# Loads alternating between the queues of SP and ACT in a decode kernel that streams 346 MB

## The chip, the cores and the metric

The kernel runs on one core of a Trainium2 chip. The core has five engines: TensorE (PE) for matrix products, VectorE (DVE), ScalarE (ACT), GpSimd (POOL) and SyncE (SP), which here only issues transfers. Each engine works through its own list of instructions in order and waits on semaphores for the others. Transfers between the large memory and the on-chip memory are issued by an engine into a queue that belongs to it (SP's is q1 in the profile, ACT's is q10) and are carried out by 16 DMA engines that all queues share. A transfer of 128 rows raises its semaphore by 16 when all its rows have landed.

The metric is the device time of one execution in microseconds (us). Lower is better.

## The reference

One token is decoded. Its vector x (1024 numbers) goes through two branches, and a scalar gate mixes them:

```
g = sigmoid(sum(x * gate_w))
a = attention(x): q = x @ wq; 32 query heads share 4 key/value heads,
                  65536 cached keys and values of 128 numbers each;
                  softmax(q k / sqrt(128)) v, then @ wo
b = x + sigmoid(x @ w_r) * ((silu(x @ w_gate) * (x @ w_up)) @ w_down)
out = g * a + (1 - g) * b
```

Everything is float32. The caches of keys and values are 4 x 65536 x 128 numbers each, 134 MB apiece; the weights are the rest. Each number is used for one token only, so the work per byte is small.

## The kernel before

All large inputs are laid out by the host as one stream of 42 loads, in the order of use. Each of the 4 groups (one key/value head with its 8 query heads) has 9 loads of 8 MB: 128 partitions with one contiguous row of 64 KB each. A load holds two units: `wq` and the key chunk 0, then key chunks 1 to 7, then value chunks 0 to 7, then `wo`, 18 units in 9 loads. Six loads of 128 rows of 56 KB follow for the feed-forward branch (gate, up, down); the last two are cut into eight pieces of falling size (`ENDS`).

Three buffers (`stream`, `BUFS = 3`) take the loads in turn. SP walks the loads in order: load i goes to buffer i % 3 and, from the fourth on, waits until PE is done with the load that was there. PE says so by counting up the semaphore `marked`; `MARK` gives the count of each named point. `LAST` names the point that frees each of a group's nine loads: `s0` (key chunk 0 done) for the first, then `s2`, `s4`, `s6`, `v0` (value chunk 0), `v2`, `v4`, `v6`, `w`.

The order of work in one group, all of it written out by hand:

- PE multiplies x by `wq` (L310, mark `q`), DVE copies the result (L229), PE turns it with a small matrix `half` (L317, mark `qt`), DVE spreads it into `qp` (L233).
- For each key chunk c PE computes scores (L326, mark `s`c), ACT copies them out (L171), DVE takes the maximum (L240).
- Maximum over the group (L332 on PE), ACT computes eight exponentials (L176), DVE transposes them (L255), PE multiplies by the values (L338, marks `v`c).
- PE sums and multiplies by `wo` (L345 to L355, marks `o` and `w`).

Before the first group, ACT issues two small loads: `xk` (L161: x, gate_w and w_r, 128 rows of 96 bytes) and, after POOL has cleared its destination (semaphore `x0`), `x_row` (L163: x once more as two rows of 2 KB). DVE waits for `xk`, prepares `xp` and the dot products (L205 to L208); then, in this order in its list, it computes the gates (L211 to L215), waits for `x_row` (semaphore `x2`), scales it (L217), makes the small selection matrices `sel`, `sel4`, `half`, `halves`, `sel8`, `nsel` (L220 to L226), and only then enters the loop over the groups, which begins with the copy of the queries (L229). The scaled `x_row` itself is used first at the end of the attention (L265).

At the end the gate and up products, their activation (ACT, L179) and the down product follow, and SP stores the output.

Of the kernel before, what the change touches and what calls it, by code (L numbers as in the profile page):

```python
# [10 lines left out]
G = 4  # L11
# [16 lines left out]
PER = UNITS // 2  # L28
BUFS = 3

TAIL = 14336
NTAIL = 3 * KB * F // TAIL

ENDS = {NTAIL - 2: [8 * D, TAIL], NTAIL - 1: [6 * D, 10 * D, 12 * D, 13 * D, 13 * D + 768, TAIL]}

PIECES = [(0, 192), (192, NQ)]

EARLY = 24

# [4 lines left out]
MARK = {m: i + 1 for i, m in enumerate(MARKS)}  # L44

LAST = ["s0", "s2", "s4", "s6", "v0", "v2", "v4", "v6", "w"]
# [5 lines left out]
def gated_mix_kernel(nc, x, vecs, heads, ffn, out):  # L52
# [21 lines left out]
    pe, act, dve, pool, sp = nc.tensor, nc.scalar, nc.vector, nc.gpsimd, nc.sync  # L74

    stream = [nc.alloc_sbuf_tensor(f"st{b}", [P, 2 * CH], F32, align_bytes=256)[:, :] for b in range(BUFS)]
# [24 lines left out]
    gate = sig[:, 0:1]  # L101
# [12 lines left out]
    sems = {n: nc.alloc_semaphore(n) for n in names}  # L114
    nums = sorted(s.num for s in sems.values())
    assert nums == list(range(nums[0], nums[0] + len(nums)))


    ends = []
    for i in range(G * PER + NTAIL):  # L120
        b = i % BUFS
        if i >= BUFS:
            g, l = divmod(i - BUFS, PER)
            sp.wait_ge(sems["marked"], MARK[f"{LAST[l]} {g}" if g < G else ["gate 0", "gate 1", "up 0"][l]])
        if i < G * PER:
            sp.dma_start(stream[b], heads[i]).then_inc(sems[f"ld{b}"], 16)
        elif i - G * PER not in ENDS:
            sp.dma_start(stream[b][:, :TAIL], ffn[i - G * PER]).then_inc(sems[f"ld{b}"], 16)
        else:
            cuts = ENDS[i - G * PER]  # L130
            for c0, c1 in zip([0] + cuts, cuts):
                sp.dma_start(stream[b][:, c0:c1], ffn[i - G * PER, :, c0:c1]).then_inc(sems[f"end{len(ends)}"], 16)  # L132
                ends.append((i, c0, c1))
# [23 lines left out]
    def tell(ins, name):  # L157
        acted.append(name)
        return ins.then_inc(sems["acted"])

    act.dma_start(xk, vecs).then_inc(sems["x1"], 16)  # L161
    act.wait_ge(sems["x0"], 1)
    act.dma_start(  # L163
        x_row[:64:32, :], x.rearrange("(f n) -> f n", f=2)
# [3 lines left out]
    for g in range(G):  # L168
        for c in range(NCH):
            act.wait_ge(sems["marked"], MARK[f"s{c} {g}"])  # L170
            tell(act.activation(scores[:, c, :], ps_s[c % 2], AF.Copy), f"s{c} {g}")  # L171
        act.wait_ge(sems["d2a"], g + 1)
        for c in range(NCH):
            t = scores[:, c, :]
            tell(
                act.activation(t, t, AF.Exp, bias=nb, scale=SCALE, accum_out=sums[:, c : c + 1]), f"e{c} {g}"  # L176
            )
    act.wait_ge(sems["marked"], MARK["gate 1"])
    tell(act.activation(hid.rearrange("p (e n) -> p e n", e=2), ps_f[:, :, :FN], AF.Exp, scale=-1.0), "hid")  # L179
    act.wait_ge(sems["marked"], MARK["first"])  # L180
    c0, c1 = PIECES[0]
    tell(act.activation(fin[:, c0:c1], banks[0][:, : c1 - c0], AF.Copy), "first")
# [11 lines left out]
    def after(mark):  # L194
        dve.wait_ge(sems["marked"], MARK[mark])
# [82 lines left out]
    after("last")  # L278
    c0, c1 = PIECES[1]
    dve.tensor_copy(fin[:, c0:c1], banks[1][:, : c1 - c0]).then_inc(sems["d2s"])  # L280
# [8 lines left out]
    def take(name, n=1):  # L289
        pe.wait_ge(sems[name], n).then_inc(sems[name], -n)  # L290
# [106 lines left out]
    for b in range(EARLY, FB):  # L397
        if b == EARLY + 2:
            take("d2p")
        for bank, (c0, c1) in zip(banks, PIECES):  # L400
            n = c1 - c0
# [45 lines left out]
```

## Time and profile before

| | |
|---|---|
| runs of the kernel | 805.68, 805.76, 806.18 us; median 805.76 |
| the profiled execution | 805.78 us, of which the span of the profile is 804.5 us |
| read from the large memory | 346.05 MB, 430 GB/s over the span |
| busy PE, DVE, ACT, POOL | 407.5, 72.3, 44.8, 2.5 us |

Times in the profile are microseconds from the start of the span. "SPq" and "ACTq" are the issues of transfers by these engines; their time is that of the issue alone, not of the transfer. In an instruction's row, the bracket at the end gives the idle time of its engine before it and what ended it. A row that stands for several instructions has their count (x32). The granted clock is the share of its full speed that TensorE was given.

### The profile page before, as it was taken

The numbers are of one execution on the slowest core, as the hardware profiler recorded it, in microseconds if no ns is written. First come the engines' busy times: TensorE is split into PE (matmuls) and PEld (weight loads), VectorE is DVE, ScalarE is ACT, GpSimd is POOL, SyncE is SP. The second block draws the span as 40 slices with busy tenths as digits, with TensorE's granted clock in tenths as the row PEclk, the third lists the DMA queues.
The fourth block names the chain that finished last, engine by engine and source line by source line (L and its number), as shares of the span: only waits on it lengthen the run. The fifth ranks groups of instructions, "written<-read, shape, count | busy, mean of one in ns | idle before, by whom it ended". The sixth has DMA issues, their size and how long they took to land. (4 is left out here: it accounts for less than half of the span.)

```text
span 804.5 us, 6124 instructions
## 1 busy us (share of the span) xinstructions
PE 407.5 (51%) x2826; PEld 122.0 (15%) x2826; DVE 72.3 (9%) x135; ACT 44.8 (6%) x100; POOL 2.5 (0%) x13
## 2 busy tenths in 40 slices
PE   0544464455654564545544454456444545464466
PEld 0211111111111121111111111112111111121122
DVE  0200010000000020000100110000000100000310
ACT  0000030000000030000000110000000300000000
POOL 1000000000000000000000000000000000000000
PEclk9977767768767677677877586777776866787778
DMA  9999999999999999999999999999999999999998
GB/s 418 417 418 466 415 424 460 417 428 453 420 430 450 424 431 446 427 430 446 427 430 443 430 430 443 430 431 430 440 433 427 443 430 430 429 448 426 439 413 342
DMA packets 7078, 346.20 MB, mean 430 GB/s; under 512 B 918, under 2 KB 1050, under 8 KB 1308
## 3 DMA queue, kind: packets, MB, share of 16 engines
q1 hardware_dynamic: 6920, 346.04, 99.4%
q8 instruction: 8, 0.13, 0.1%
q10 hardware_dynamic: 148, 0.02, 0.0%
q14 instruction: 2, 0.02, 0.0%
HBM read 346.05 MB, written 0.00 MB: 430 GB/s over the span
## 5 line engine op out<-in xcount | busy, mean ns | idle before, releaser
L326 PE MATMUL ps_u<-st,qp 128*32 128x512 f32 x1024 | 152.5, 759 | 149.1 <-PEq L290 149.1
L338 PE MATMUL acc<-st,pt 128*32 128x512 f32 x1024 | 152.3, 757 | 144.1 <-PEq L290 144.1
L338 PEld LDWEIGHTS acc<-st,pt 128*32 128x32 f32 x1024 | 43.5, 135 | 250.0 <-issue 250.0
L326 PEld LDWEIGHTS ps_u<-st,qp 128*32 128x32 f32 x1024 | 41.4, 135 | 256.3 <-issue 256.3
L171 ACT ACTIVATE s<-ps_u 128x512 f32<-128x512 f32 x32 | 19.1, 597 | 560.4 <-PE ps_u L326 560.4
L240 DVE TENSOR_REDUCE mx<-s 128x1 f32<-128x512 f32 x32 | 22.0, 686 | 284.2 <-ACT s L171 284.2
L255 DVE STREAM_TRANSPOSE pt<-s 128x512 f32<-128x512 f32 x32 | 22.7, 711 | 198.0 <-PE acc L338 194.4
L310 PE MATMUL ps_u<-st,xp 128*32 128x512 f32 x128 | 23.3, 893 | 22.1 <-PEq L290 22.1
L382 PE MATMUL ps_u<-st,xp 128*32 128x448 f32 x128 | 17.1, 703 | 16.9 <-PEq L290 16.9
L382 PE MATMUL ps_f<-st,xp 128*32 128x448 f32 x128 | 16.8, 691 | 13.3 <-PEq L290 13.3
L176 ACT ACTIVATE s<-s,nb 128x512 f32<-128x512 f32 x32 | 22.6, 708 | 10.4 <-DVE nb L250 10.4
L392 PE MATMUL att<-st,s 128*32 128x512 f32 x96 | 14.9, 776 | 7.5 <-DMA st<-in_ffn 4.9
L355 PE MATMUL att<-st,op 128*32 128x512 f32 x128 | 14.6, 594 | 2.4 <-PEq L290 2.4
L301 PE MATMUL ps_m<-dsum,ones 128*128 128x2 f32 x2 | 0.6, 350 | 23.5 <-PEq L290 23.5
L310 PEld LDWEIGHTS ps_u<-st,xp 128*32 128x32 f32 x128 | 5.9, 158 | 40.1 <-issue 40.1
L382 PEld LDWEIGHTS ps_u<-st,xp 128*32 128x32 f32 x128 | 5.3, 139 | 28.6 <-issue 28.6
L259 DVE COPY s<-acc 128x512 f32<-128x512 f32 x4 | 2.8, 692 | 71.6 <-PE acc L338 71.6
L382 PEld LDWEIGHTS ps_f<-st,xp 128*32 128x32 f32 x128 | 5.2, 135 | 25.1 <-issue 25.1
L229 DVE COPY s<-ps_u 128x512 f32<-128x512 f32 x4 | 2.8, 692 | 53.5 <-PE ps_u L310 53.5
L179 ACT ACTIVATE s<-ps_f 128x896 f32<-128x896 f32 x1 | 0.9, 917 | 105.4 <-PE ps_f L382 105.4
L392 PEld LDWEIGHTS att<-st,s 128*32 128x32 f32 x96 | 3.7, 134 | 18.6 <-issue 10.7
L332 PE MATMUL ps_m<-md,ones 128*128 128x128 f32 x8 | 1.8, 311 | 8.2 <-PEq L290 8.2
(69 smaller groups left out, 68.9 us busy)
## 6 DMA issues: line engine op xcount, KB each, us to landing
st<-in_ffn SPq DMA_DIRECT2D x4, 7168.0 KB, 43.3
st<-in_ffn SPq DMA_DIRECT2D x2, 3072.0 KB, 37.1
st<-in_ffn SPq DMA_DIRECT2D x1, 4096.0 KB, 34.9
st<-in_ffn SPq DMA_DIRECT2D x1, 2048.0 KB, 36.9
st<-in_ffn SPq DMA_DIRECT2D x1, 1024.0 KB, 38.9
st<-in_heads SPq DMA_DIRECT2D x36, 48.1
st<-in_ffn SPq DMA_DIRECT2D x1, 512.0 KB, 39.7
st<-in_ffn SPq DMA_DIRECT2D x1, 384.0 KB, 40.2
```

The source lines that it names most:

```text
L171: tell(act.activation(scores[:, c, :], ps_s[c % 2], AF.Copy), f"s{c} {g}")
L176: act.activation(t, t, AF.Exp, bias=nb, scale=SCALE, accum_out=sums[:, c : c + 1]), f"e{c} {g}"
L229: to_pe(dve.tensor_copy(q_sb, ps_s[0]))
L240: ins = dve.tensor_reduce(mx[:, c : c + 1], scores[:, c, :], AX.X, ALU.max)
L255: to_pe(dve.transpose(pts[:, c % 2, :], scores[:, c, :]))
L259: to_pe(dve.tensor_copy(o_sb, acc.rearrange("p (s d) -> p s d", s=4)))
L310: ins = pe.matmul(ps_s[0][32 * j : 32 * j + 32, :], xp[:, k, :], unit(0)[:, k * D + f * 512 : k * D + (f + 1) * 512], start=(k < 2), stop= ...
L326: ins = pe.matmul(ps_s[c % 2][32 * j : 32 * j + 32, :], qp[:, 32 * s : 32 * s + 32], unit(1 + c)[:, (4 * s + j) * 512 : (4 * s + j + 1) * ...
L338: ins = pe.matmul(acc[32 * j : 32 * j + 32, :], pts[:, c % 2, 32 * m : 32 * m + 32], unit(1 + NCH + c)[:, m * 512 : (m + 1) * 512], start= ...
L355: ins = pe.matmul(att[32 * j : 32 * j + 32, :], op[:, h, :], unit(UNITS - 1)[:, h * D + f * 512 : h * D + (f + 1) * 512], start=False, sto ...
L382: ins = pe.matmul(ps[32 * j : 32 * j + 32, e, :FN], xp[:, k, :], tail((i * KB + k) * F + (2 * j + e) * FN, FN), start=(k == 0), stop=(k == ...
L392: ins = pe.matmul(att[32 * j : 32 * j + 32, :], hp[:, 32 * b : 32 * b + 32], tail(2 * KB * F + b * D + f * 512, 512), start=(b < 2), stop= ...
```

## The change

The loads are dealt out to two queues. Of the first 39 loads (`ONE = 39`) the even ones stay with SP and the odd ones, 1, 3, ..., 37, are issued by ACT. Loads 39 to 41, with all pieces of the end, stay with SP. Buffers, order of use, semaphores and points of release are the same; both queues wait for the same marks as before, load by load.

In ACT's list an odd load's issue stands at these places: load 1 between the issues of `xk` and `x_row`, without a wait; a load that is released by a mark `s`c directly after ACT's copy of that chunk, whose wait for the mark serves both; a load released by `v`c or `w` after the eight exponentials of its group, with a wait for the mark of its own.

```diff
+ONE = G * PER + NTAIL - 3
...
+    def release(i):
+        g, l = divmod(i - BUFS, PER)
+        return f"{LAST[l]} {g}" if g < G else ["gate 0", "gate 1", "up 0"][l]
+
+    def load(queue, i):
+        b = i % BUFS
+        if i < G * PER:
+            queue.dma_start(stream[b], heads[i]).then_inc(sems[f"ld{b}"], 16)
+        else:
+            queue.dma_start(stream[b][:, :TAIL], ffn[i - G * PER]).then_inc(sems[f"ld{b}"], 16)
+
+    on_act = {release(i): i for i in range(3, ONE, 2)}
...
     for i in range(G * PER + NTAIL):
         b = i % BUFS
+        if i < ONE and i % 2 == 1:
+            continue
         if i >= BUFS:
-            g, l = divmod(i - BUFS, PER)
-            sp.wait_ge(sems["marked"], MARK[f"{LAST[l]} {g}" if g < G else ["gate 0", "gate 1", "up 0"][l]])
-        if i < G * PER:
-            sp.dma_start(stream[b], heads[i]).then_inc(sems[f"ld{b}"], 16)
-        elif i - G * PER not in ENDS:
-            sp.dma_start(stream[b][:, :TAIL], ffn[i - G * PER]).then_inc(sems[f"ld{b}"], 16)
+            sp.wait_ge(sems["marked"], MARK[release(i)])
+        if i - G * PER not in ENDS:
+            load(sp, i)
         else:
...
     act.dma_start(xk, vecs).then_inc(sems["x1"], 16)
+    load(act, 1)
     act.wait_ge(sems["x0"], 1)
     act.dma_start(
         x_row[:64:32, :], x.rearrange("(f n) -> f n", f=2)
...
             act.wait_ge(sems["marked"], MARK[f"s{c} {g}"])
             tell(act.activation(scores[:, c, :], ps_s[c % 2], AF.Copy), f"s{c} {g}")
+            if f"s{c} {g}" in on_act:
+                load(act, on_act.pop(f"s{c} {g}"))
...
+        for name in [n for n in on_act if n.endswith(f" {g}")]:
+            act.wait_ge(sems["marked"], MARK[name])
+            load(act, on_act.pop(name))
```

More of the change, by code (lines that the diff above doesn't have):

```diff
@@ L177, in gated_mix_kernel @@
             )
+        for name in [n for n in on_act if n.endswith(f" {g}")]:
+            act.wait_ge(sems["marked"], MARK[name])
+            load(act, on_act.pop(name))
+    assert not on_act
     act.wait_ge(sems["marked"], MARK["gate 1"])
```

## The prediction

> **What bounds the kernel now.** I read the page first: the span, the DMA shares and the queues.
>
> ```profile
> span 804.5 us, 6124 instructions
> PE 407.5 (51%) x2826; PEld 122.0 (15%) x2826; DVE 72.3 (9%) x135; ACT 44.8 (6%) x100; POOL 2.5 (0%) x13
> DMA packets 7078, 346.20 MB, mean 430 GB/s; under 512 B 918, under 2 KB 1050, under 8 KB 1308
> q1 hardware_dynamic: 6920, 346.04, 99.4%
> q10 hardware_dynamic: 148, 0.02, 0.0%
> xk<-in_vecs ACTq DMA_DIRECT2D x1, 12.0 KB, 22.0
> ```
>
> The queue of SP (q1) carries all but 0.02 MB, and its packets fill 99.4% of the time of the 16 DMA engines, while TensorE, the busiest engine, is at half. The kernel is one long transfer, and only two things can change its time: the rate, and a pause. Rows of the windows view (start:end, length, busy of PE, PEld, DVE, ACT, POOL, granted clock, DMA share, GB/s) give the rate in the middle:
>
> ```profile
> 260.00:360.00 100.00, 52.78 (x347) 15.23 (x339) 9.83 (x19) 7.54 (x19) 0.00 (x0) 0.71 1.00 433
> 460.00:560.00 100.00, 53.81 (x370) 16.57 (x370) 7.99 (x15) 5.30 (x16) 0.00 (x0) 0.73 1.00 433
> ```
>
> Share 1.00: there is no idle DMA time there to win. The chain that ended last (start, us, what) says the same of the end: the last load, then 3.2 us of small matmuls and a copy.
>
> ```profile
> 760.52 38.89 DMA st<-in_ffn
> 799.41 0.04 issue
> ...
> 802.38 0.23 DVE s L280
> ```
>
> Now the start, which the change touches first; the DMA view for the first 12 us, then the timeline.
>
> ```profile
> DMA packets 112, 4.20 MB, mean 350 GB/s; under 512 B 48, under 2 KB 48, under 8 KB 48
> q1 hardware_dynamic: 64, 4.19, 86.4%
> q10 hardware_dynamic: 48, 0.00, 0.3%
> ```
>
> q1's 64 packets of 4.19 MB are 64 KB each: one row of one partition. In the same time q10, the queue of ACT, has passed 48 packets of xk. Per engine that is four large and three small in turn: **an engine takes one packet from each queue alternately, however different their sizes.** That is why 12 KB of xk need 22.0 us: each engine has eight of its rows, and each waits out a 64 KB packet of the first load. This rule is the base of what follows.
>
> ```profile
> 0.74 1.34 SPq L126 DMA_DIRECT2D st<-in_heads  x3
> 1.29 1.06 ACTq L163 DMA_DIRECT2D x_row<-in_x  x1
> 22.88 0.17 DVE L205 COPY xp<-xk 128x8 f32<-128x8 f32 x1 [22.88 <-DMA xk<-in_vecs]
> 25.74 5.09 PE L310 MATMUL ps_u<-st,xp 128*32 128x512 f32 x32
> 27.52 0.49 DVE L217 TENSOR_SCALAR x_row<-x_row,rest 128x512 f32<-128x512 f32 x1 [2.42 <-DMA x_row<-in_x]
> 29.09 0.17 DVE L226 TENSOR_SCALAR nsel<-sel 128x8 f32<-128x8 f32 x1
> 30.98 0.69 DVE L229 COPY s<-ps_u 128x512 f32<-128x512 f32 x1 [1.72 <-PE ps_u L310]
> 33.24 3.64 PE L326 MATMUL ps_u<-st,qp 128*32 128x512 f32 x32 [0.40 <-PEq L290]
> 36.94 0.33 SPq L126 DMA_DIRECT2D st<-in_heads  x1
> 36.94 0.60 ACT L171 ACTIVATE s<-ps_u 128x512 f32<-128x512 f32 x1 [12.63 <-PE ps_u L326]
> 42.09 8.88 PE L326 MATMUL ps_u<-st,qp 128*32 128x512 f32 x64 [5.21 <-PEq L290]
> 47.60 0.60 ACT L171 ACTIVATE s<-ps_u 128x512 f32<-128x512 f32 x1 [10.06 <-PE ps_u L326]
> 63.04 8.65 PE L326 MATMUL ps_u<-st,qp 128*32 128x512 f32 x64 [12.06 <-PEq L290]
> 82.34 9.23 PE L326 MATMUL ps_u<-st,qp 128*32 128x512 f32 x64 [10.65 <-PEq L290]
> ```
>
> Three loads are issued at once. DVE waits for x_row (L217) before it does anything for the queries; mark s0, at 36.94, frees the first buffer and lets load 3 go. The matmuls at 42.09, 63.04 and 82.34 start as loads 1, 2 and 3 land, so a load takes 82.34 - 63.04 = 19.3 us, a turn of one 64 KB packet per engine 19.3 / 8 = 2.41 us.
>
> **The change part by part.**
>
> 1. *Where the bytes travel.* 19 of 42 loads move from q1 to q10. Bytes, packet sizes and engines stay. Two loads in flight now share the engines packet by packet, each at half its rate. With engines already full this moves landings, not their sum: 0 us, as long as some packet is always waiting. The price of a change of queue is nowhere in the trace by itself; the nearest row is load 0, which ran with eight xk packets between its own:
>
> ```profile
> st<-in_heads SPq DMA_DIRECT2D x1, 21.9
> ```
>
> (DMA view, issues of the first microsecond: issue to landing.) Eight turns are 19.3, so everything else, the start of an empty queue and the eight switches, is 2.6 us, at most 0.3 per switch; below nothing by no row. Since q1's share is 1.00 with packets back to back, I take 0 and leave 1.5 us on both sides in the range.
>
> 2. *Issue time.* SP is relieved of 19 issues of 0.33 us and ACT gets them; SP spent most of its life waiting, ACT is at 6%. 0 us.
>
> 3. *x_row moves behind load 1, and this is the term that counts.* ACT now issues xk, load 1, x_row. Queue q10 is then eight turns of xk, eight of load 1, and only then x_row's two packets. xk still alternates with load 0 and is seen at 22.88. From there loads 2 (q1) and 1 (q10) alternate for 16 turns, 16 x 2.41 = 38.6 us, and x_row follows. L217 starts at 22.88 + 38.6 = 61.5 instead of 27.52. Lower end 60.9, upper 63.0, the start by load 2 in the row of 63.04, since the same three loads' bytes are then in.
>
> Behind that wait on DVE are sel, half, sel8, nsel and the copy of the queries (L229), which PE waits for before the first key chunk. So load 0 can't be freed, and loads 1 and 2 have landed too: **all three buffers are full, both queues empty, the DMA engines stop.** The step after step:
>    - L217 to the end of L226: 29.26 - 27.52 = 1.75, so L229 starts near 63.3 (q's matmuls, done at 30.8, no longer hold it).
>    - L229 to mark s0: 36.94 - 30.98 = 5.96: 69.2.
>    - PE has then been idle 30 us. A chunk of keys took 36.94 - 33.24 = 3.70 after running matmuls, and 47.60 - 42.09 = 5.51 after 5.2 us of idling, when the granted clock read
>
> ```profile
> 37.00:42.00 5.00, 0.00 (x0) 0.70 0.97 419
> 42.00:44.00 2.00, 1.91 (x12) 0.50 1.06 459
> ```
>
>    (same windows view, PE alone), and up to 6.40 after a longer idle (first two rows below). So plus 1.8, ends 0 and 2.7: 71.0. I take the 5.51, since the four query matmuls L317 run ahead and begin the warming.
>    - Load 3 is now ACT's, issued in its program after the copy of s0: plus 0.60 if the issue waits for the copy, 0 if not. I take 0.60: 71.6.
>    - Issue to landing in empty queues, 21.9 as load 0: 93.5, and 0.4 for PE to start: 93.9. (Load 4 joins it a few us later and delays its landing, not the bytes.) Before, PE started on load 3 at 82.34: **11.6 us late**, and everything behind it with it, since the transfer has no slack to give back.
>
> 4. *ACT's waits.* In the half of values, ACT waits for v0, v2 and so on after its eighth exponential; it has no other work there until the next s0.
>
> ```profile
> 101.75 6.33 PE L326 MATMUL ps_u<-st,qp 128*32 128x512 f32 x32 [10.17 <-PEq L290]
> 108.15 0.60 ACT L171 ACTIVATE s<-ps_u 128x512 f32<-128x512 f32 x1 [15.91 <-PE ps_u L326]
> 116.91 0.19 ACT L176 ACTIVATION_READ_ACCUMULATOR s<-s,nb 128x1 f32 x1
> 118.92 0.33 SPq L126 DMA_DIRECT2D st<-in_heads  x1
> ```
>
> The exponentials end at 117.1, mark v0 comes at 118.9: ACT is there in time. 0 us.
>
> 5. *The steady part.* Load 3 has a lead of two to three turns on load 4, so landings come about 13 and 26 us apart instead of 19.3. A load is held longest round the softmax, 118.92 - 101.75 = 17.2 us; with 0.6 for ACT and 2.6 to start an empty queue, 20.4. When a load lands, of the two behind it about 11 or 13 turns of 16 are still to come, 26 us or more. No second pause: 0 us.
>
> 6. *The end.* Loads 39 to 41 all go by SP in order behind load 38; load 37 is through long before. The last load lands as late as the pause made it. 0 us.
>
> Sum: +11.6 us on the profiled execution, 805.78 us (span 804.5), which stands 0.02 above the median of 805.76. **817.4 us.**
>
> **Rivals.** A measurement of this kernel tells about 0.2% (1.6 us) from nothing.
>
> *No change, 805.8 us.* If x_row's packets passed ahead of load 1, or DVE's late start were covered by a load still in flight, the transfer would have no pause. Against it: q10 was served in order before (xk seen at 22.88, x_row at 27.52, two turns later), and nothing is left to issue before s0. The Trainium skill, "DMA: Bandwidth & Descriptors", section "Issuing engines are not separate DMA queues", holds that transfers from different engines interleave on the same 16 DMA engines and that spreading them saves only issue time, which would be this rival. The trace agrees with the interleaving (48 packets of q10 among 64 of q1); what a small transfer pays that stands behind a load in its queue, the section does not say. Chance 0.05.
>
> *Faster.* Turns from two queues are packed more densely than from one. To break even it must win 11.6 us over 39 x 8 = 312 turns, 37 ns of 2.41 us, 1.5%; to end 0.2% below, 13.2 us, 42 ns, 1.7%: 802 to 804 us. The windows show 433 GB/s at full share with one queue, and 1.7% would be 440. The same page, "Where 436 GB/s comes from", sets a ceiling of 435 GB/s, by which at most 0.5%, 4 us, could be won and the time would be 813 at best; the two rows of 433 lie under it. Chance 0.03.
>
> *A second pause.* If the stagger of step 5 is lost and only eight turns (19.3 us) are left when the load with the softmax lands, each of four groups stops for 20.4 - 19.3 = 1.1 us: 817.4 + 4.4 = 822. For it: nothing fixes the stagger. Against it: any load issued late makes the other queue lead, which restores one. Chance 0.08.
>
> **How the numbers follow.** The forecast, one pause of 9 to 14 us, has 0.84. Its own range: low, PE warm (-1.8), issue beside the copy (-0.6) and switches at -1.5: 813.5; high, 6.40 for the chunk (+0.9), x_row at 63.0 (+1.5), switches at +1.5: 821.3. With the second pause taken in, 813.5 to 822. Slower 0.92 (forecast and second pause), same 0.05, faster 0.03.
>
> **What would show it.** Right: x_row's scaling on DVE starts between 60.9 and 63 instead of 27.5, waiting for its DMA; DMA share near zero from about 61 to 72; the first key chunk takes 5 us or more at half clock; q10 with about 160 MB; middle windows at 433 GB/s; the last chain unchanged and some 11 us later. Wrong: x_row's scaling near 27 or 42; load 3 issued near 37; zero slices later in the span; a rate above 435 or below 430 GB/s in the middle.

## The result, and the profile after

The changed kernel takes 819.50 us (median of 6 runs, 818.38 to 819.82) against 805.83 us (6 runs, 805.68 to 806.18): a ratio of 1.0166, interval 1.0156 to 1.0177, or 13.7 us more. The profiled execution took 819.70 us. The range was 813.5 to 822.0, the forecast 817.4: direction and cause as foreseen, the size 2.1 us short.

The page of the changed kernel (lines have moved by 22 in DVE's, ACT's and PE's parts):

```profile
span 818.4 us, 6124 instructions
DMA  9994999999999999999999999999999999999998
GB/s 411 410 410 193 423 430 439 414 452 420 448 423 445 426 445 420 449 423 445 423 439 432 420 452 420 452 420 448 423 445 426 442 426 445 416 441 438 424 425 339
q1 hardware_dynamic: 4184, 187.70, 53.1%
q10 hardware_dynamic: 2884, 158.35, 44.8%
```

Half the loads did move to q10, and the two queues' shares sum to 97.9% where q1 alone had 99.4%. What is missing lies in one place: the fourth of 40 slices (61.4 to 81.8 us) is at 4 tenths, all others are as full as before. The windows view resolves it (columns as before: start:end, length, busy of PE, PEld, DVE, ACT, POOL, granted clock, DMA share, GB/s):

```profile
20.00:60.00 40.00, 6.65 (x42) 1.88 (x42) 1.14 (x8) 0.17 (x1) 0.00 (x0) 0.68 0.97 419
60.00:62.00 2.00, 0.00 (x0) 0.00 (x0) 0.61 (x2) 0.00 (x0) 0.00 (x0) 0.50 0.01 2
62.00:64.00 2.00, 0.01 (x1) 0.04 (x1) 1.70 (x7) 0.00 (x0) 0.00 (x0) 0.50 0.00 0
64.00:72.00 8.00, 7.60 (x36) 3.31 (x40) 0.21 (x1) 0.00 (x0) 0.00 (x0) 0.51 0.01 2
72.00:74.00 2.00, 2.00 (x24) 0.67 (x20) 0.67 (x1) 0.60 (x1) 0.00 (x0) 1.00 1.26 426
...
360.00:460.00 100.00, 51.12 (x374) 16.19 (x370) 6.45 (x13) 3.31 (x6) 0.00 (x0) 0.79 1.00 433
460.00:560.00 100.00, 48.51 (x352) 14.49 (x344) 10.21 (x21) 7.21 (x19) 0.00 (x0) 0.78 1.00 433
```

From about 60.7 to 73.7 no byte of a load moves. In the middle of the span two queues carry 433 GB/s at share 1.00, the same figures as one queue before. The timeline shows who holds the transfer:

```profile
22.94 0.18 DVE L227 COPY xp<-xk 128x8 f32<-128x8 f32 x1 [22.94 <-DMA xk<-in_vecs]
25.80 4.45 PE L332 MATMUL ps_u<-st,xp 128*32 128x512 f32 x32
61.39 0.49 DVE L239 TENSOR_SCALAR x_row<-x_row,rest 128x512 f32<-128x512 f32 x1 [36.23 <-DMA x_row<-in_x]
63.15 0.69 DVE L251 COPY s<-ps_u 128x512 f32<-128x512 f32 x1
63.98 1.84 PE L339 MATMUL ps_m<-half,s 128*128 128x2 f32 x8 [33.73 <-PEq L312]
66.22 20.15 PE L348 MATMUL ps_u<-st,qp 128*32 128x512 f32 x160 [0.40 <-PEq L312]
72.70 0.60 ACT L187 ACTIVATE s<-ps_u 128x512 f32<-128x512 f32 x1 [48.33 <-PE ps_u L348]
72.71 0.33 ACTq L128 DMA_DIRECT2D st<-in_heads  x1
107.21 3.64 PE L348 MATMUL ps_u<-st,qp 128*32 128x512 f32 x16 [20.84 <-PEq L312]
```

xk arrives as before. x_row, at 27.52 before, now comes at 61.39, after 36.23 us in which DVE did nothing; the copy of the queries, the query matmuls and the first key chunk follow one another, and load 3 goes out at 72.71 instead of 36.94. The chain that ended last has the same last stage, some 14 us later (start, us, what):

```profile
772.16 41.15 DMA st<-in_ffn
813.31 0.04 issue
...
816.30 0.23 DVE s L302
```

### The profile page after: what moved, and what is told of

Same layout as the page of the kernel before. It is cut to its first block, busy times and chain, and to the rows that moved or that the text cites. A ratio compares the mean times of both kernels' runs of the same rounds, so it can differ in the third digit from the quotient of the medians.

```text
span 818.4 us, 6124 instructions
## 1 busy us (share of the span) xinstructions
PE 391.2 (48%) x2826; PEld 118.7 (14%) x2826; DVE 72.4 (9%) x135; ACT 44.8 (5%) x100; POOL 2.5 (0%) x13
## 5 line engine op out<-in xcount | busy, mean ns | idle before, releaser
L360 PE MATMUL acc<-st,pt 128*32 128x512 f32 x1024 | 147.0, 735 | 148.1 <-PEq L312 148.1
L348 PE MATMUL ps_u<-st,qp 128*32 128x512 f32 x1024 | 145.3, 729 | 139.7 <-PEq L312 139.7
L360 PEld LDWEIGHTS acc<-st,pt 128*32 128x32 f32 x1024 | 41.2, 132 | 251.1 <-issue 251.1
L332 PE MATMUL ps_u<-st,xp 128*32 128x512 f32 x128 | 21.9, 844 | 28.9 <-PEq L312 28.9
L339 PE MATMUL ps_m<-half,s 128*128 128x2 f32 x32 | 4.9, 275 | 36.4 <-PEq L312 36.4
L404 PE MATMUL ps_u<-st,xp 128*32 128x448 f32 x128 | 14.1, 597 | 10.7 <-PEq L312 10.7
L339 PEld LDWEIGHTS ps_m<-half,s 128*128 128x128 f32 x32 | 4.7, 225 | 40.2 <-issue 40.2
```

The lines of the kernel that those rows point to most:

```text
L332: ins = pe.matmul(ps_s[0][32 * j : 32 * j + 32, :], xp[:, k, :], unit(0)[:, k * D + f * 512 : k * D + (f + 1) * 512], start=(k < 2), stop= ...
L339: ins = pe.matmul(ps_m[:, 2 * e : 2 * e + 2], q_sb[:, e * DH : (e + 1) * DH], half, start=True, stop=True)
L348: ins = pe.matmul(ps_s[c % 2][32 * j : 32 * j + 32, :], qp[:, 32 * s : 32 * s + 32], unit(1 + c)[:, (4 * s + j) * 512 : (4 * s + j + 1) * ...
L360: ins = pe.matmul(acc[32 * j : 32 * j + 32, :], pts[:, c % 2, 32 * m : 32 * m + 32], unit(1 + NCH + c)[:, m * 512 : (m + 1) * 512], start= ...
L404: ins = pe.matmul(ps[32 * j : 32 * j + 32, e, :FN], xp[:, k, :], tail((i * KB + k) * F + (2 * j + e) * FN, FN), start=(k == 0), stop=(k == ...
```

## The experiments

The theory: the loss is one pause, made by x_row standing behind load 1 in ACT's queue while DVE holds everything for it. Rival A: alternating the loads costs by itself, a little at each change of queue. Rival B: the pause comes from loads 1 and 2 landing together, whatever x_row does.

**x_row ahead of load 1.**

```diff
     act.dma_start(xk, vecs).then_inc(sems["x1"], 16)
-    load(act, 1)
     act.wait_ge(sems["x0"], 1)
     act.dma_start(
         x_row[:64:32, :], x.rearrange("(f n) -> f n", f=2)
     ).then_inc(sems["x2"], 16)
+    load(act, 1)
```

> As the changed kernel, but ACT issues xk, x_row, load 1 in this order (load 1 after x_row instead of before it). Theory (the whole loss is the one pause, made by x_row standing behind load 1): x_row is scaled near 27.5 us, mark s0 falls near 37, no slice of the DMA row is empty, and the time is that of the kernel before, 805.8 us, within 1.6. Rival A (alternating the loads costs by itself, through the change of queue at each of some 300 turns): a part of the 13.7 us stays, so over 808 us, with lower GB/s in the middle windows. Rival B (loads 1 and 2 landing together near 60 empties the queues, whatever x_row does): a pause near 60 us stays and the time is 812 to 819.

Measured: 805.89 us (11 runs, 805.74 to 806.56) against 805.86; ratio 1.0001, interval 0.9992 to 1.0010. Two rows of its page:

```profile
DMA  9999999999999999999999999999999999999998
q10 hardware_dynamic: 2884, 158.35, 45.5%
```

and three of its timeline:

```profile
27.43 0.49 DVE L239 TENSOR_SCALAR x_row<-x_row,rest 128x512 f32<-128x512 f32 x1 [2.33 <-DMA x_row<-in_x]
37.48 0.34 ACTq L128 DMA_DIRECT2D st<-in_heads  x1
61.56 16.78 PE L348 MATMUL ps_u<-st,qp 128*32 128x512 f32 x128 [24.15 <-PEq L312]
```

All 19 loads still go through q10, the alternation is whole, and the loss is gone: **rival A falls, to within 0.1%.** Load 1 lands near 61 instead of 42, PE idles 24.15 us for it, and that costs nothing, since load 0's buffer was free at 37 and bytes kept coming: rival B falls too.

**Load 1 alone on ACT,** all others on SP as in the kernel before.

```diff
+        if i == 1:
+            continue
         if i >= BUFS:
...
     act.dma_start(xk, vecs).then_inc(sems["x1"], 16)
+    act.dma_start(stream[1], heads[1]).then_inc(sems["ld1"], 16)
     act.wait_ge(sems["x0"], 1)
```

> As the kernel before, all loads on SP, but load 1 alone is issued by ACT, ahead of x_row. Theory: the same start as in the changed kernel, x_row scaled near 61.4 us, DMA empty from 60.7 to about 73, and from there one queue: the whole loss is there, 818.5 to 820.5 us. Rival A (the alternation costs): only part of the loss, under 815 us. Rival B (loads 1 and 2 landing together): as the theory.

Measured: 819.48 us (818.22 to 820.07), ratio 1.0162, interval 1.0147 to 1.0178. One load of 42 on the other queue, ahead of x_row, carries the whole loss, as its timeline shows:

```profile
61.60 0.49 DVE L220 TENSOR_SCALAR x_row<-x_row,rest 128x512 f32<-128x512 f32 x1 [36.48 <-DMA x_row<-in_x]
72.42 31.48 SPq L128 DMA_DIRECT2D st<-in_heads  x4
```

**x_row late, but not waited for.** x_row stays behind load 1; DVE waits for it and scales it after the last group.

```diff
-    dve.wait_ge(sems["x2"], 16)
-    dve.tensor_scalar_mul(x_row, x_row, rest[:, 0:1])
...
+    dve.wait_ge(sems["x2"], 16)
+    then(dve.tensor_scalar_mul(x_row, x_row, rest[:, 0:1]))
     after(f"w {G - 1}")
```

> As the changed kernel, x_row still behind load 1 in ACT's queue, but DVE waits for it and scales it after the fourth group, just ahead of its use, instead of ahead of the selection matrices. Theory (the wait at the head of DVE's list is the link): x_row still lands near 61, mark s0 falls near 36, no pause, 805.8 us within 1.6 although DVE gets 0.5 us of work late. Rival A: over 808 us. Rival B: a pause near 60 us and 812 to 819 us.

Measured: 805.90 us (11 runs, 805.66 to 806.57), ratio 1.0000, interval 0.9991 to 1.0009. Its timeline:

```profile
26.28 0.17 DVE L246 TENSOR_SCALAR nsel<-sel 128x8 f32<-128x8 f32 x1
36.91 0.33 ACTq L128 DMA_DIRECT2D st<-in_heads  x1
```

The transfer order is that of the changed kernel; only the place of the wait differs, and load 3 goes out at 36.91. So two things together make the pause: a small transfer queued behind a large one, and a wait for it at the head of an in-order engine. Either taken away gives all of it back.

**x_row half as late.** Load 1 is cut into halves with x_row between them.

```diff
-    load(act, 1)
+    act.dma_start(stream[1][:, :CH], heads[1, :, :CH]).then_inc(sems["h1"], 16)
     act.wait_ge(sems["x0"], 1)
...
     ).then_inc(sems["x2"], 16)
+    act.dma_start(stream[1][:, CH:], heads[1, :, CH:]).then_inc(sems["ld1"], 16)
...
     dve.wait_ge(sems["x2"], 16)
+    dve.wait_ge(sems["h1"], 16)
```

> As the changed kernel, but load 1 is cut into two transfers of half the columns, with x_row between them in ACT's queue: first half, x_row, second half. (DVE waits for the first half as well, where it waits for x_row.) Theory (what counts is when x_row lands against the time at which the other bytes run out): the first half has eight packets of 32 KB, 1.21 us a turn, between eight of 64 KB, so x_row lands after 22 + 8 x 3.62 = 51 us and DVE scales it at 51.5 to 52.5; s0 follows 11.3 us later, at 63 to 64; the bytes still run out at 60.7 and load 3 starts 1.1 us after s0, so the pause is 3.4 to 4.4 us and the time 809.5 to 811 us. Rival (the pause comes from loads 1 and 2 filling all buffers together, whatever the time of x_row): 819 us, or no pause at all and 805.8 us.

Measured: 809.76 us (809.48 to 810.01), ratio 1.0047, interval 1.0030 to 1.0064. Its timeline:

```profile
51.99 0.48 DVE L241 TENSOR_SCALAR x_row<-x_row,rest 128x512 f32<-128x512 f32 x1 [26.77 <-DMA st<-in_heads]
63.02 0.33 ACTq L128 DMA_DIRECT2D st<-in_heads  x1
```

The bracket names the first half of load 1, for which DVE waits as well in this run: by the trace it landed at 51.69, x_row at 51.61, so the two are late together. Scaled 9.40 us earlier than in the changed kernel, x_row lets load 3 go 9.69 us earlier, and the time falls by 819.50 - 809.76 = 9.74 us: past the point where the other bytes run out, each microsecond of lateness is a microsecond of time. The rival's times, 819 or 805.8 us, are both out.

**What the halved clock costs.** Three kernels give PE multiplications of zeros to do while x_row is awaited, so that the first key chunk doesn't meet a rested array.

```diff
-    for j in range(4):
+    for n in range(140):
+        j = n % 4
         pe.matmul(att[32 * j : 32 * j + 32, :], op[:, 0, :], zeros, start=True, stop=False, skip_group_check=True)
```

> As the changed kernel, but PE does 140 instead of 4 multiplications of zeros ahead of the first product of queries, some 33 us of work without use that ends at about 62 us, so that it comes to the first key chunk without the idle time of 33 us. Theory (of the pause, what PE loses by its halved clock is 0.8 us in the four query matmuls and 2.8 us in the first key chunk): mark s0 moves from 72.7 to 69.1 us and the time from 819.5 to 815.9 us. Rival (the chunk was slow for another reason, such as reading buffers while nothing moves): s0 stays near 72.7 and the time near 819.5. If the zeros end after 63.2 us, all is late by the excess; the profile tells.

Measured: 819.74 us (818.87 to 820.08), as the changed kernel. The zeros ended too early: the product of queries was over at 59.45, and the clock fell in the pause before the query matmuls:

```profile
60.00:62.00 2.00, 0.00 (x0) 0.89 0.01 2
62.00:64.00 2.00, 0.00 (x0) 0.50 0.00 0
64.00:66.00 2.00, 1.84 (x8) 0.50 0.00 0
```

(Windows view, PE alone: busy, clock, DMA share, GB/s.) It says nothing on the chunk. The second run has 153 multiplications in the same place.

> As the run with 140 multiplications of zeros, with 153: there the last product of queries ended at 59.45 us, PE idled 4.5 us until the query matmuls at 64, and the granted clock was back at 0.50; 13 more at 0.23 us put the end near 62.4, with about 1.5 us of idling left. Theory (clock): the four query matmuls take 1.0 us instead of 1.84, the first key chunk 3.7 instead of 6.5, mark s0 comes at 69.1 instead of 72.7 us, and the time is 815.9 us. Rival (another reason): s0 near 72.7, 819.5 us.

Measured: 818.47 us (817.73 to 819.32), ratio 1.0159, interval 1.0143 to 1.0176. The same windows view of PE, and the timeline:

```profile
62.00:64.00 2.00, 0.78 (x3) 1.00 0.00 0
64.00:66.00 2.00, 1.60 (x12) 0.71 0.00 0
66.00:68.00 2.00, 2.00 (x13) 0.50 0.03 8
68.00:70.00 2.00, 2.00 (x24) 0.93 0.00 0
```

```profile
63.99 1.05 PE L340 MATMUL ps_m<-half,s 128*128 128x2 f32 x8 [1.22 <-PEq L312]
65.44 18.75 PE L349 MATMUL ps_u<-st,qp 128*32 128x512 f32 x160 [0.40 <-PEq L312]
70.52 0.60 ACT L187 ACTIVATE s<-ps_u 128x512 f32<-128x512 f32 x1 [46.14 <-PE ps_u L349]
```

The query matmuls are at full speed (1.05 us instead of 1.84), then the clock falls all the same for some 3 us. s0 comes at 70.52, 2.18 us earlier than in the changed kernel. The third run brings the zeros closer, with the first group written out ahead of the loop:

```diff
-    with pe.Fori(0, G):
+    def group(warm):
...
         mark(ins, "q")
+        for n in range(warm):
+            pe.matmul(acc[32 * (n % 4) : 32 * (n % 4) + 32, :], op[:, 0, :], zeros, start=True, stop=True)
         take("d2p")
...
+    group(146)
+    marks = marks[:1]
+    with pe.Fori(0, G - 1):
+        group(0)
```

> As the changed kernel, but the first group is written out ahead of PE's loop over the other three, and has 146 multiplications of zeros (into a bank not yet in use) between its product of queries and the wait for their copy; they run from about 30 to 63.5 us, so PE idles half a microsecond instead of 1.2 (run with 153 ahead of the product, where the clock still fell to 0.50 for part of the first key chunk and s0 came at 70.5). Theory (clock): clock at 1.00 through the chunk, s0 near 69.1 us, time 815.9 us. If the clock falls again for a part, s0 between 69.1 and 70.5 and 816 to 818 us. Rival (the chunk is slow for another reason): s0 at 72.7, 819.5 us.

Measured: 819.24 us (5 runs, 817.32 to 819.41), ratio 1.0158, interval 1.0144 to 1.0172. Its timeline:

```profile
63.95 1.02 PE L341 MATMUL ps_m<-half,s 128*128 128x2 f32 x8 [1.72 <-PEq L312]
65.38 10.06 PE L350 MATMUL ps_u<-st,qp 128*32 128x512 f32 x76 [0.40 <-PEq L312]
70.77 0.60 ACT L187 ACTIVATE s<-ps_u 128x512 f32<-128x512 f32 x1 [46.42 <-PE ps_u L350]
```

The zeros ended at 62.2, 1.72 us before the query matmuls, not half a microsecond, and s0 and the time both lie above the ranges that were expected for a clock that falls for a part. Taken together: with the clock up for part of the way the same work is about 2 us shorter; in the second run 0.79 of its 2.18 us lie in the query matmuls (1.05 instead of 1.84) and 1.40 in the chunk (5.08 from its start to s0 instead of 6.48). The full 3.6 us of the expectation were in no run, as in none the clock stayed up throughout.

The kept traces settle the rest. By their record of the clock it rose from 0.50 to 1.00 at 71.87 us in the changed kernel; in the second run it was 0.50 from 64.85 to 68.27, in the third from 65.53 to 68.94. If time at 0.50 is counted half, the first key chunk, from its start to s0, comes to 3.66, 3.67 and 3.69 us in these three, next to 3.70 in the kernel before, where the clock was at 1.00. So the clock is all of what the chunk lost, and nothing is left for the rival. In the medians the 2 us are hardly seen (818.47 and 819.24 against 819.50), as the kernels with the long pause scatter over 1.2 to 2.1 us from run to run, those without one over 0.5 to 0.9. In the profiled executions the second run keeps 1.97 of its 2.18 us, the third 0.65 of 1.93; in the third each DMA engine was busy for 802.0 us on average instead of 801.2 in the changed kernel, and why stays open.

No experiment gave a kernel faster than the one before; the best two equal it.

## Why the prediction was right, and where its size was off

- *Where the bytes travel (step 1, 0 us, 1.5 us either way):* right. With x_row ahead of load 1, alternation measures 1.0001; the rival of denser packing is out as well: from 160 to 760 us the windows of 100 us average 433.7 GB/s in the kernel before and 433.5 in the changed one. (Single windows read 430 to 437 in both, so the prediction's sign of a rate above 435 can't be read from one of them.) The ceiling of 435 GB/s from the Trainium skill, "DMA: Bandwidth & Descriptors", section "Where 436 GB/s comes from", agrees with the 433 GB/s of one queue and of two.
- *Issue time (2), ACT's waits (4), the steady part (5), the end (6), each 0 us:* right together, by the same run and by the full slices behind the fourth. Load 3, alone for a while and then at half rate, was used at 107.21, 24.9 us later than before, of which only 13.9 stayed in the time; the other 11 were a changed order of landing. The stagger of step 5 held only at first: by the trace the loads behind load 3 landed 15 and 24 us apart in turn (forecast 13 and 26), and from about 240 us on 18 to 22 us apart.
- *x_row (3):* L217's work at 61.39, forecast 61.5; L229's at 63.15, forecast 63.3. The rule of alternate packets, read from 48 packets of xk among 64 of load 0, gave the time 34 us ahead to 0.1 us.
- *From L229 to s0 with the clock:* this is the term that was mis-sized. Forecast 5.96 + 1.8 = 7.76 us, measured 72.70 - 63.15 = 9.55. The prediction said that the query matmuls "begin the warming". They did not: they took 1.84 us instead of 1.02, and the clock stood at 0.51 all the way from 64 to 72, so the chunk took 6.48 us, next to the 6.40 that had been put at the end of the range. The 5.51 were taken from a chunk in which the clock rose 3.70 us after its start (at 45.79); here it rose 5.65 us after the start (at 71.87).
- *ACT's issue after its copy:* forecast 0.60 us, measured 0.01 (72.70 and 72.71): ACT's queue does not wait for the copy ahead of it in the list.
- *The sum:* with these two it is 72.71 + 21.9 + 0.4 - 82.34 = 12.7 us. The profiled execution is 13.9 us longer than the one before. The kept trace accounts for all of it: between the last packet of the first three loads and the first of load 3 each of the 16 DMA engines stood idle for 13.25 us on average, and that first packet took 3.03 us on average instead of 2.42, together 13.9. The 1.2 us left lie most likely in the point from which the prediction counted, PE's start on load 3 before (82.34): of the 16 shares of load 3, one per DMA engine, 15 had landed by 80.63 then and the last at 82.05, so the start that the sum took for the end of the bytes was that of one late engine. That this lag of 1.4 us makes the 1.2 us fits the numbers, but no run tests it.
- *The rivals:* "no change" describes the two kernels in which one half of the cause is missing. The section "Issuing engines are not separate DMA queues" of the same page of the Trainium skill, by which spreading transfers over engines saves issue time only, agrees with the runs once nothing small stands behind a load: 1.0001. The second pause did not come, though the stagger that was to keep it away faded; why it still did not come stays open.

## What to carry to other kernels

Before loads are moved to another engine's queue, list what is already in that queue and who waits for it: a 4 KB transfer behind an 8 MB load arrives when the load does, and the load itself is slowed by the other queue. In a kernel whose DMA share is 1.00, landing times may move by 20 us for nothing, and only an empty moment costs; so look for the first wait whose lateness keeps a buffer from being freed. And put a wait on an in-order engine next to the use of the data, not at the head of the list.

## What the runs showed of the hardware that was not expected

The clock did not rise as soon as there was work. In the changed kernel PE was busy for 7.60 of the 8 us from 64 to 72, and the granted clock was 0.51 on average through them. In the run with 153 multiplications it fell from 1.00 to 0.50 after 35 us of steady work and an idle time of only 1.22 us, 0.86 us into the small matmuls that followed; in the kernel before, a like sequence (the product of queries, 0.99 us of idling, L317, 0.40 us) was followed by a chunk at full speed, 3.64 us. So a short interruption may or may not cost the clock.

The traces' record of the clock has a pattern that bears on it: in all nine profiled executions every stretch at one clock lasts 3.41 us or a whole multiple of it, but for the last, which the end of the span cuts off. The clock changed at the ends of such steps alone. In the run with 153 multiplications the step that ended with the fall at 64.85 held 1.3 us of large matmuls; in the kernel before the interruption was split between two steps that met at 32.14, with 2.1 and 2.3 us of large matmuls in them, and the clock stayed up. That it matters how an interruption lies in these steps is a reading of the traces; no run was made to test it.
